# Attention and a gated feed-forward block in one kernel: whole-array value matmuls for two batches, loads tied to TensorE's place in the list, and a new list

## The chip, the cores and the metric

The kernel runs on one core of one Trainium2 chip. The metric is the time of one execution on the device in microseconds (us). A core has five engines that work through queues of their own: TensorE (PE in the profile; its weight loads are listed apart as PEld), VectorE (DVE), ScalarE (ACT), GpSimd (POOL) and SyncE (SP). Matrix results land in PSUM, everything else on the core lies in SBUF. Transfers are carried by 16 DMA engines and are issued here from three places: POOL's queue (loads, which also turn float32 into bfloat16), SP's queue (transposing transfers and stores), and ACT's (one load and one store).

## The reference

```python
def _attn_ref(q, k, v, beacon_k, beacon_v):
    # q, k, v: (8, 8, 576, 64); beacons: (8, 8, 16, 64)
    k_all = np.concatenate([beacon_k, k], axis=2)
    v_all = np.concatenate([beacon_v, v], axis=2)
    scores = scale * np.matmul(q, k_all.transpose(0, 1, 3, 2))
    ...
    scores = np.where(causal, -1000000000.0, scores)
    scores = scores - scores.max(-1, keepdims=True)
    a = np.exp(scores)
    a /= a.sum(-1, keepdims=True) + 1e-09
    return np.matmul(a, v_all).astype(np.float32)

def _moe_ref(x, w_gate, w_val, w_out):
    # x: (4608, 512); w_gate, w_val: (512, 1536); w_out: (1536, 512)
    g = x @ w_gate
    silu = g * (1.0 / (1.0 + np.exp(-g)))
    val = x @ w_val
    return (silu * val @ w_out).astype(np.float32)
```

`scale` is 1/8. The mask is causal over the 576 tokens; the 16 beacon keys in front of them are seen by every query. The attention output, with the eight heads side by side, is the `x` of the feed-forward block.

## The kernel before, in words

**Attention** goes by batch (8) and by pair of heads (4 per batch). The 592 keys are cut into five blocks of 128 rows (`NKT`), the 576 queries into five blocks (`QBLOCKS`). Scores are made transposed, keys on the partitions and queries along the row, in four units per pair (`UNITS`), each into one PSUM slot of two banks, one bank per head. `exponent` (line 323) takes a unit to SBUF as bfloat16, in tiles `p0` to `p2`; `mask` (line 330) zeroes the diagonal blocks on DVE or POOL, unless the scores were masked already by a few extra matmuls. `pv` (line 348) multiplies the exponentials with the values `vb`, which have a column of ones as a 65th column, so that the sum of a row falls out beside its result. `normalize` (line 366) divides on DVE and writes `x`.

**Queries and keys** must have the head dimension on the partitions. Batches 0 to 2 (`NPE`) are loaded as runs of rows, regrouped (`regroup`), transposed on TensorE (`turn`) and copied out of PSUM (`turned_copy`). Batches 3 to 7 are loaded in row blocks and transposed by transfers from SP (`dma_transposes`, line 272, ten per batch). `x` of batch 0 is transposed on TensorE (`x_turn`), that of the others by five or six transfers from SP (`x_transpose`, line 392).

**Feed-forward** goes by chunk of 512 tokens (9) and block of 128 of the 1536 features (12). `gate_value` (line 404) makes gate and value of a block in one slot of two banks, in two pieces of 8 matmuls; `tanh`, `act1` and `act2` build the activation on ACT and DVE; `project` (line 444) multiplies with `w_out`, two matmuls a piece; `evacuate` copies the result to SBUF and stores it.

**Row halves.** Nearly every matmul of TensorE goes through `halves` (line 112): it uses 64 of the 128 rows of the array, and two in a row use the two halves and run together, each writing a bank of its own. When a bank that one half has written is to be written by the other, a `nop` on TensorE waits for the last matmul of that slot before (the "gate"). `pv` is called twice for a pair. The first call takes the upper half of the keys for one head and the lower half for the other; the second call swaps them. Each call issues 30 matmuls of 64 rows by 128 columns of weights with 65 moving columns: for each of the 15 combinations of query block and key block, two.

**The order** is written out by hand in strings (`plan`, line 615), one letter for each piece of work; `piece` (line 560) turns a letter into instructions, and each engine takes its own in that order. The letters that matter here: S/s scores, without and with masking matmuls, E exponential, D/M mask on DVE/POOL, P/p first and second call of `pv`, R normalize, T transpose, c/C regroup, K/k/Q/q copies of transposes, X/Y/y batch 0's `x`, V `x_transpose`, t one transfer of `dma_transposes`, g gate matmuls of the first block as soon as parts of `x` are there, G/H the two gate pieces, a/1/2 activation, F one `project` piece, O/o `evacuate` on DVE/ACT, h two filling matmuls that are issued with the next scores or values, and l the next load. Loads are issued from POOL in the order of the list `loads` (119 of them); POOL also works on the masks M, in the same queue. A load waits until its buffer is free, and, since eight semaphores are used in turn for POOL's transfers, until the load eight places earlier has landed. The buffers `qk`, `vb`, `qT` and `kT` are double.

Of the kernel before, what the change touches and what calls it, by code (L numbers as in the profile page):

```python
# [55 lines left out]
def kernel(  # L56
# [52 lines left out]
    def give(key):  # L109
        spare.append(held.pop(key))  # L110

    def halves(key, bank, row, o, l, r, start, stop, turn=False):

        at = (held[key], bank)
        was = writers.get(at)
        if was is not None and was[0] != row:
            last = max((w for (i, _), w in writers.items() if i == at[0]), key=lambda w: w[2])
            if was[3]:
                gate = nc.tensor.nop()
                tc.add_manual_dep(  # L120
                    gate.ins,
                    last[1],
                    mybir.DependencyInfo(mybir.DependencyClass.Sync, mybir.DependencyReason.DATA),
                    reason="one bank, two row halves",
                )
            for other, w in writers.items():
                if other[0] == at[0]:
                    writers[other] = (w[0], w[1], w[2], False)
        if turn:
            ins = nc.tensor.transpose(o, l, r)  # L130
        else:
            ins = nc.tensor.matmul(o, lhsT=l, rhs=r, start=start, stop=stop)  # L132
# [408 lines left out]
    loads = [  # L541
        weights[1], vl[0][2], vl[0][5], vl[0][3], vl[0][0], vl[0][4], vl[0][1], run_loads(1)[1], weights[0],
        run_loads(1)[0], lambda: beacon_load(1), vl[1][4], weights[3], vl[1][3], weights[2], weights[5],
        vl[1][1], vl[1][2], weights[4], weights[7], vl[2][0], weights[6], vl[1][5], vl[1][0],
        lambda: load_wo(1), lambda: load_wo(0), run_loads(2)[1], run_loads(2)[0], lambda: beacon_load(2),
        vl[2][1], vl[2][2], vl[2][4], vl[2][3], vl[2][5], kl[3][0], kl[3][1], ql[3][0], kl[3][2], ql[3][1],
        kl[3][3], ql[3][2], kl[3][4], ql[3][3], kl[3][5], ql[3][4], kl[4][0], kl[4][1], ql[4][0], kl[4][2],
        ql[4][1], kl[4][3], ql[4][2], kl[4][4], ql[4][3], kl[4][5], ql[4][4], vl[3][0], vl[3][1], vl[3][2],
        vl[3][3], vl[3][4], vl[3][5], kl[5][0], kl[5][1], ql[5][0], kl[5][2], ql[5][1], kl[5][3], ql[5][2],
        kl[5][4], ql[5][3], kl[5][5], ql[5][4], vl[4][0], vl[4][1], vl[4][2], vl[4][3], vl[4][4], vl[4][5],  # L550
        kl[6][0], kl[6][1], ql[6][0], kl[6][2], ql[6][1], kl[6][3], ql[6][2], kl[6][4], ql[6][3], kl[6][5],
        ql[6][4], vl[5][0], vl[5][1], vl[5][2], vl[5][3], vl[5][4], vl[5][5], kl[7][0], kl[7][1], ql[7][0],
        kl[7][2], ql[7][1], kl[7][3], ql[7][2], kl[7][4], ql[7][3], kl[7][5], ql[7][4], vl[6][0], vl[6][1],
        vl[6][2], vl[6][3], vl[6][4], vl[6][5], vl[7][0], vl[7][1], vl[7][2], vl[7][3], vl[7][4], vl[7][5],
    ]
# [59 lines left out]
    plan = [
        "0TclqKTlKhslEsQlEsclcTElsKTEslKElhhsQlQEhhslEslEslEslEslhhhhhPElspEsRPESplPREspERsXlEXDXyPyYpgRl",
        "cXlcyTlcTqgKqTKlGaqKlSHE1G2acslHE1T2aGQklG1lS2HElDGaDSH1E2lSaHDE1G2aGlD1SlHE2HaDlG1al2Gl1SHE2HaD",
        "G1al2G1SHE2saDPHE12pasRPlEp1SFEF2FFFFRsFEslFFEDSFFPEspEDsFRFlFEFFclPcTplcqTKFFlkFFRTqFlFkFFcVSlq",
        "FOFFEFlTOFFFKlqSFFEDSlFFFEMSFlFFFEDSlFESDlFPFEMSplFERFSFMtFFlESOGolEGMDtSHMElGtaDlS1HEtl2HaltG1a",
        "M2Gtl1SHEl2tGlaDl1StHEl2HatMGl1at2Gl1SHE2HlaGM1a2G1SHE2HaDG1a2SHEt1MGa2tP1P2tplpRlSHtElRSaFtlFFE",  # L620
        "1SFlF2FtEFSFlDPDFEDtSlpEDSFRlFtFESFMFPlEtSFpMEDSFltFERSFlFFEFSlFFMDFESVFMFFlFoPlFoFpEMSRFESFlFFF",
        "DESDFPEFMSplFRFESMFEFFFDlSFDEStPlFFEpltGRlGtlSHEltGal1HVl2Hal1Gal2FFH1l2lGaOloG1MSMH2EMGlaDSt1lH",
        "E2lHtaGl1at2Gl1MStHE2HaMtG1at2G1SHE2MGa1SHE2HaMG1al2Gl1SHlE2HlaDG1al2Gl1SHlE2HlaG1la2Gl1SlHE2MGa",
        "D1PH2paGRH1Ga2H12Ga1SHE2HaDG1a2G1SHE2HaDS1aFFF2EFFF1SFEtFMF2FFMFPtFFpStRFESFFFFtEDSFFFFEMSFtFOFF",
        "oFFDFEFFDFFtFFPPtppRSlFtEFFlFRSFEStlFFFFElSFVFFFlEOSFoFPlESFMpMFERSMFFFESFDFFDPDEMSFDEpSFRFEMSFF",
        "FESDtFFFFPEMtFDGptGRHtGat1H2Hta1Gat2FFH1o2GatOG1SH2EtGaDtS1HE2HtaMG1a2G1SHE2HaMG1a2G1SHE2GaD1SHE",
        "2HaMS1FaFFE2FFFF1FSF2ESFFFDPEDFFMpSRlFESFlFFFVEDSlFFFFEDlSFFFFoOlFFDPElFDFpSRFESFFFFEDSPFEFMpSFR",
        "FEMSFEFFDFSFMEGGMSHEHaMG1a2FFH1G2a1G2FHOGOa1SHE2MGa1FFFF2FFHGa1H2Ha1Ga2FFH12Ga1G2HGa1FFFF2HFaFH1",
        "FaF2FFF1FFF2FFFOFFFFOPPppRSFEFFFRSFMESFFVPEDSFpFEDSFMESRFFFFEMSFFFFEDSFFOFFoFPDESFDEpSFRFEMSFFFE",
        "SDFFPFEDGMpGRHGa1H2Ha1Ga2FFH12Ga1G2HGa1FFFF2FFFPFFpoOHRGaV1H2Ga1H2Ga1FH2Ha1Ga2FFF1G2HHa1Ga2FFH12",  # L630
        "Ga1G2HGa1H2Ha1Ga2FFH12Ga1G2HGa1H2Ha1Ga2FFF1G2FHGa1FFFF2FFFFFFFFFOHOFaFFG1F2FFFFFFFHGa1FFFF2FFFFF",
        "FFFFoOFFFFFFHGa1H2Ha1Ga2FFF1G2FFHGa1H2Ha1Ga2FFH12Ga1G2FFFFFHGa1H2Ha1Ga2FFF1G2FFHooGaFF1FFF2FFFFF",
        "FFHFaFH1FaF2FFF1FFF2FFFoFFFoFFFFFFFFFFFFFFFFFFFFFOFFOFFFFFFFFFoFFFFoFFFFFFFFoO",
    ]
# [40 lines left out]
```

## Time and profile before

| what | value |
|---|---|
| median of 3 runs (range) | 388.66 us (385.17 to 393.87) |
| profiled execution, its own time | 392.0 us |
| its span (first to last instruction) | 389.5 us |
| mean granted TensorE clock | 0.969 of full |
| TensorE matmul busy | 360.5 us, 5338 matmuls |
| VectorE / ScalarE / GpSimd busy | 227.9 / 186.0 / 122.7 us |
| packets of loads (POOL's queue) | 95,424, 18.85 MB |
| packets of transposes and stores (SP's queue) | 48,224, 19.92 MB |
| packets of instructions (TensorE's) | 41, 0.67 MB |

The page gives the busy time of each engine, the span in 40 equal slices with a digit for the busy share of each (and rows for the granted clock and the DMA engines), the share of each DMA queue, and the chain of work that ended last: the way back from the last instruction, at each step to what released it. In the lists of waits a line names the waiting engine and its line, then what ended the wait, then microseconds in total, how often, and the longest. "Issue" stands where the profile shows nothing that was waited for. A table of windows gives, for each stretch of time, its length and mean, the busy microseconds of each engine with the number of instructions, the clock, the DMA share (over 1 when packets overlap) and the gigabytes per second moved.

### The profile page before, as it was taken

The page shows a single profiled execution, that of the slowest core. Times are in us where ns is not written, and L with a number is a line of the kernel's source. Part 1 is how long each engine was busy: PE and PEld are TensorE (multiplying, and loading weights), DVE is VectorE, ACT ScalarE, POOL GpSimd, SP SyncE. Part 2 cuts the span into 40 slices and gives each one's busy share as a digit, 9 for nine tenths or more (in the row PEclk, how much of TensorE's full clock was granted, in tenths as well). Part 3 has the DMA queues.
Part 4 walks back from the last instruction along what each step waited for, and adds up shares of the span by engine and source line. Part 5 has one row for each costly group of instructions (what it writes and reads, how often), then busy time and mean ns, then how long its engine had stood idle before and what let it go on. Part 6 is the DMA issues. An engine that isn't in the chain of part 4 may idle for free.

```text
span 389.5 us, 12163 instructions
## 1 busy us (share of the span) xinstructions
PE 360.5 (93%) x5338; PEld 206.5 (53%) x5338; DVE 227.9 (59%) x413; ACT 186.0 (48%) x271; POOL 122.7 (31%) x197
## 2 busy tenths in 40 slices
PE   6659999999977689999998999999999999999996
PEld 3455456555544435555665556555665555555543
DVE  4524887747952337778444875477646767456521
ACT  2833667776464526545473567633552332122321
POOL 8754526095664747550171015200100000000000
PEclk9885999999998989999999999999999999999999
DMA  8999999399999999990799618910330400110112
GB/s 152 157 194 194 203 176 126 42 153 164 145 128 142 172 115 185 123 109 0 133 104 160 139 17 71 112 56 2 89 84 2 108 10 0 56 56 2 54 56 109
DMA packets 143989, 39.90 MB, mean 102 GB/s; under 512 B 130368, under 2 KB 139328, under 8 KB 143936
## 3 DMA queue, kind: packets, MB, share of 16 engines
q0 software_dynamic: 95424, 18.85, 66.1%
q1 hardware_dynamic: 48224, 19.92, 29.8%
q8 instruction: 41, 0.67, 0.8%
q10 hardware_dynamic: 288, 0.36, 0.3%
q14 instruction: 12, 0.10, 0.1%
HBM read 38.27 MB, written 9.44 MB: 122 GB/s over the span
## 4 chain that ended last, share of the span: by engine, by line
PE 82%; DMA 6%; issue 4%; POOL 3%; DVE 2%; SPq 2%; ACT 1%; POOLq 0%
PE gv_ps L132 45%; PE o_ps L132 23%; PE pv_ps L132 7%; PE s_ps L132 5%; DMA qT<-qk 2%; DMA vb<-in_v_dram 2%; DMA xT<-x 2%; SPq L274 1%; POOL vb L180 1%; DVE o_sb L224 1%; PE t_ps L130 1%; PE xt_ps L386 1%; POOL qk L171 1%; SPq L397 1%; ACT o_sb L222 0%
## 5 line engine op out<-in xcount | busy, mean ns | idle before, releaser
L132 PE MATMUL gv_ps<-xT,wg 64*128 64x512 bf16 x864 | 201.9, 380 | 6.5 <-issue 4.0
L132 PE MATMUL gv_ps<-xT,wv 64*128 64x512 bf16 x864 | 203.3, 380 | 0.0
L327 ACT ACTIVATE p<-s_ps 128x992 bf16<-128x992 f32 (+2 forms) x128 | 105.5, 865 | 72.2 <-PE s_ps L132 66.4
L132 PE MATMUL o_ps<-wo,hT 64*128 64x512 bf16 (+2 forms) x912 | 115.7, 368 | 2.8 <-issue 2.6
L425 ACT ACTIVATE th<-gv_ps 128x512 f32<-128x512 f32 x108 | 64.4, 596 | 90.7 <-PE gv_ps L132 88.3
L429 DVE SCALAR_TENSOR_TENSOR u<-th,gv_ps 128x512 f32<-128x512 f32 x108 | 73.9, 684 | 57.6 <-ACT th L425 57.3
L132 PEld LDWEIGHTS <-wg 64*128 64x128 bf16 x864 | 80.2, 95 | 49.0 <-PE gv_ps L132 3.8
L132 PEld LDWEIGHTS <-wv 64*128 64x128 bf16 x864 | 79.6, 95 | 44.5 <-issue 5.4
L436 DVE SCALAR_TENSOR_TENSOR hT<-gv_ps,u 128x512 bf16<-128x512 f32 x108 | 74.7, 691 | 3.7
L132 PEld LDWEIGHTS <-hT 64*128 64x128 bf16 x912 | 47.0, 94 | 38.0 <-issue 3.5
L340 POOL TENSOR_SCALAR_AFFINE_SELECT p<-p 128x256 bf16<-128x256 bf16 (+2 forms) x62 | 23.3, 396 | 116.9 <-ACT p L327 100.3
L132 PE MATMUL pv_ps<-vb,p 64*128 64x65 bf16 x1920 | 41.7, 193 | 8.8 <-issue 6.5
L132 PEld LDWEIGHTS <-p 64*128 64x128 bf16 x1920 | 38.8, 96 | 18.1 <-issue 7.6
L132 PE MATMUL s_ps<-qT,kT 64*128 64x80 bf16 (+4 forms) x384 | 46.1, 285 | 2.3 <-DMA qT<-qk 1.3
L180 POOL DMA_DIRECT2D vb<-in_v_dram x40 | 33.8, 854 | 19.0 <-DMA qk<-in_k_dram 4.1
L372 DVE RECIPROCAL rec<-pv_ps 128x10 f32<-128x10 f32 x32 | 7.0, 219 | 45.0 <-PE pv_ps L132 44.9
L336 DVE TENSOR_TENSOR p<-p,upper 128x256 bf16<-128x256 bf16 (+2 forms) x71 | 19.0, 287 | 21.8 <-ACT p L327 21.5
L132 PEld LDWEIGHTS <-kT 64*128 64x128 bf16 x384 | 21.9, 96 | 17.4 <-issue 4.9
L373 DVE TENSOR_TENSOR x<-pv_ps,rec 128x640 bf16<-128x640 f32 x32 | 26.4, 824 | 1.2
L224 DVE COPY o_sb<-o_ps 128x512 f32<-128x512 f32 (+1 forms) x20 | 12.9, 666 | 20.4 <-PE o_ps L132 10.5
L180 POOL DMA_DIRECT2D qk<-in_q_dram x25 | 21.6, 864 | 3.8 <-DMA vb<-in_v_dram 2.9
L180 POOL DMA_DIRECT2D qk<-in_k_dram x25 | 21.4, 857 | 4.2 <-DMA vb<-in_v_dram 2.5
(51 smaller groups left out, 104.0 us busy)
## 6 DMA issues: line engine op xcount, KB each, us to landing
out_dram<-o_sb SPq DMA_DIRECT2D x34, 256.0 KB, 2.4
vb<-in_v_dram POOLq DMA_DIRECT2D x24, 128.0 KB, 10.6
qk<-in_q_dram POOLq DMA_DIRECT2D x20, 128.0 KB, 9.2
qk<-in_k_dram POOLq DMA_DIRECT2D x15, 128.0 KB, 8.7
wv<-in_moe_w_val_dram POOLq DMA_DIRECT2D x4, 384.0 KB, 11.7
wg<-in_moe_w_gate_dram POOLq DMA_DIRECT2D x4, 384.0 KB, 10.4
wo<-in_moe_w_out_dram POOLq DMA_DIRECT2D x2, 768.0 KB, 12.8
qk<-in_q_dram POOLq DMA_DIRECT2D x2, 576.0 KB, 12.4
```

The costliest lines, as they stand in the source:

```text
L130: ins = nc.tensor.transpose(o, l, r)
L132: ins = nc.tensor.matmul(o, lhsT=l, rhs=r, start=start, stop=stop)
L180: return nc.gpsimd.dma_start(dst[p0 : p0 + n, c, :, 0:D], src[b, :, r : r + n, :].rearrange("h j d -> j h d"))
L224: eng.tensor_copy(o, i)
L327: nc.scalar.activation(pt[n // 4 % NPT][:, :, c0 : c0 + w], ps[:, :, 0:w], ACT.Exp, scale=0.125)
L336: nc.vector.tensor_tensor(out=ap, in0=ap, in1=upper[:, None, d : d + w].to_broadcast([P, 2, w]), op=ALU.mult)
L340: nc.gpsimd.affine_select(out=ap, in_=ap, compare_op=ALU.is_ge, fill=0.0, base=d, pattern=[[0, 2], [1, w]], channel_multiplier=-1,)
L372: nc.vector.reciprocal(rec[:], o[:, :, :, D : D + 1])
L373: nc.vector.tensor_tensor(out=xs[b][:, :, P * m : P * m + P].rearrange("p c (h d) -> p h c d", d=D), in0=o[:, :, :, 0:D], in1=rec[:].to_br ...
L425: nc.scalar.activation(th[:], gvs[n][0][:, 0, :], ACT.Tanh, scale=0.5)
L429: nc.vector.scalar_tensor_tensor(out=u[:], in0=ths[n][:], scalar=1.0, in1=gvs[n][0][:, 0, :], op0=ALU.add, op1=ALU.mult)
L436: nc.vector.scalar_tensor_tensor(out=hTs[j][:, f, :], in0=gvs.pop(n)[0][:, 1, :], scalar=0.5, in1=ths.pop(n)[:], op0=ALU.mult, op1=ALU.mult)
```

## The change

Three things are changed.

*Value matmuls.* In batches 0 and 1 (`WIDE` = 2), each call of `pv` makes one head of the pair (`side`), with 15 matmuls over all 128 rows of the array and 65 moving columns, instead of 30 over 64 rows. They don't pass through `halves`, so no gate stands between the two calls.

*Loads.* `piece` notes in `passed` the newest matmul after each letter that issued one. From load number 24 on (`FREE_LOADS`), POOL first executes a `nop` that waits for the last but one entry of `passed`.

*The list.* The strings of `plan` and the order of `loads` are new. `loads` now goes by need in natural order: the six loads of the first V, two weight blocks, batch 1's K and Q, and so on. The first block's gate matmuls come in three pieces instead of two. Letters move over the whole list; the amounts of work stay the same but for small shifts between engines (58 to 62 masks D, 22 to 19 masked score units, 10 to 8 fillers).

```diff
+WIDE = 2
+
+FREE_LOADS = 24
...
+    newest = [None]
+    passed = []
...
-                gate = nc.tensor.nop()
-                tc.add_manual_dep(
...
+                after(nc.tensor.nop(), last[1], "one bank, two row halves")
...
+        newest[0] = ins.ins.name
...
         o_ps = pvs[n]
+        if b < WIDE:
+
+            side = int(second)
+            for c, (q0, _) in enumerate(QBLOCKS):
+                for t in range(c + 1):
+                    col = p_col(t, q0)
+                    ins = nc.tensor.matmul(
+                        o_ps[:, side, 68 * c : 68 * c + D + 1],
+                        lhsT=pt[n % NPT][:, side, col : col + P],
+                        rhs=vb[b % 2][:, t, 2 * m + side, 0 : D + 1],
+                        start=t == 0,
+                        stop=t == c,
+                    )
+            newest[0] = ins.ins.name
+            return
...
     loads = [
-        weights[1], vl[0][2], vl[0][5], vl[0][3], vl[0][0], vl[0][4], vl[0][1], run_loads(1)[1], weights[0],
...
+        vl[0][0], vl[0][1], vl[0][2], vl[0][3], vl[0][4], vl[0][5], weights[0], weights[1], run_loads(1)[0],
+        run_loads(1)[1], lambda: beacon_load(1), weights[2], weights[3], weights[4], weights[5], vl[1][0],
...
-    parts = [(0, [(0, 0), (1, 0), (1, 1), (0, 1), (0, 2), (1, 2)], False), (0, [(1, 3), (0, 3)], True)]
+    parts = [(0, [(0, 0), (1, 0), (1, 1), (0, 1)], False), (0, [(0, 2), (1, 2)], False), (0, [(1, 3), (0, 3)], True)]
...
         if kind == "l":
+            if n >= FREE_LOADS:
+
+                after(nc.gpsimd.nop(), passed[-2], "paced load")
             loads[n]()
...
     plan = [
-        "0TclqKTlKhslEsQlEsclcTElsKTEslKElhhsQlQEhhslEslEslEslEslhhhhhPElspEsRPESplPREspERsXlEXDXyPyYpgRl",
...
+        "0TclqKlTqKlhSEslESDlccTESlQTklESKlQESDDEhhsDEsDEslhhhhhPlEpSRPEplSXREsElYSXDlDEsPlpEDslREsyXEgly",
...
     for kind in "".join(plan):
+        before = newest[0]
         piece(kind)
+        if newest[0] != before:
+            passed.append(newest[0])
```

`after(ins, name, reason)` is a new helper that makes `ins` wait for the instruction `name`.

More of the change, by code (lines that the diff above doesn't have):

```diff
@@ L110, in give, with after @@
         spare.append(held.pop(key))
+    def after(ins, name, reason):
+        tc.add_manual_dep(
+            ins.ins,
+            name,
+            mybir.DependencyInfo(mybir.DependencyClass.Sync, mybir.DependencyReason.DATA),
+            reason=reason,
+        )
+    newest = [None]
+    passed = []
     def halves(key, bank, row, o, l, r, start, stop, turn=False):
@@ L118, in halves @@
             if was[3]:
-                gate = nc.tensor.nop()
-                tc.add_manual_dep(
[L121 to L125, printed above, removed]
+                after(nc.tensor.nop(), last[1], "one bank, two row halves")
             for other, w in writers.items():
@@ L353, in pv @@
         o_ps = pvs[n]
+        if b < WIDE:
[9 more added lines that the diff above has]
+                        stop=t == c,
+                    )
+            newest[0] = ins.ins.name
+            return
         for c, (q0, _) in enumerate(QBLOCKS):
@@ L541 @@
     loads = [
-        weights[1], vl[0][2], vl[0][5], vl[0][3], vl[0][0], vl[0][4], vl[0][1], run_loads(1)[1], weights[0],
[L543 to L551, printed above, removed]
@@ L552 @@
-        ql[6][4], vl[5][0], vl[5][1], vl[5][2], vl[5][3], vl[5][4], vl[5][5], kl[7][0], kl[7][1], ql[7][0],
-        kl[7][2], ql[7][1], kl[7][3], ql[7][2], kl[7][4], ql[7][3], kl[7][5], ql[7][4], vl[6][0], vl[6][1],
-        vl[6][2], vl[6][3], vl[6][4], vl[6][5], vl[7][0], vl[7][1], vl[7][2], vl[7][3], vl[7][4], vl[7][5],
+        vl[0][0], vl[0][1], vl[0][2], vl[0][3], vl[0][4], vl[0][5], weights[0], weights[1], run_loads(1)[0],
+        run_loads(1)[1], lambda: beacon_load(1), weights[2], weights[3], weights[4], weights[5], vl[1][0],
@@ new lines @@
+        vl[1][1], vl[1][2], vl[1][3], vl[1][4], vl[1][5], weights[6], weights[7], lambda: load_wo(0),
+        lambda: load_wo(1), lambda: beacon_load(2), run_loads(2)[0], run_loads(2)[1], vl[2][0], vl[2][1],
+        vl[2][2], vl[2][3], vl[2][4], vl[2][5], kl[3][0], kl[3][1], ql[3][0], kl[3][2], ql[3][1], kl[3][3],
+        ql[3][2], kl[3][4], ql[3][3], kl[3][5], ql[3][4], kl[4][0], kl[4][1], ql[4][0], kl[4][2], ql[4][1],
+        kl[4][3], ql[4][2], kl[4][4], ql[4][3], kl[4][5], ql[4][4], vl[3][0], vl[3][1], vl[3][2], vl[3][3],
@@ new lines @@
+        vl[3][4], vl[3][5], kl[5][0], kl[5][1], ql[5][0], kl[5][2], ql[5][1], kl[5][3], ql[5][2], kl[5][4],
+        ql[5][3], kl[5][5], ql[5][4], vl[4][0], vl[4][1], vl[4][2], vl[4][3], vl[4][4], vl[4][5], kl[6][0],
+        kl[6][1], ql[6][0], kl[6][2], ql[6][1], kl[6][3], ql[6][2], kl[6][4], ql[6][3], kl[6][5], ql[6][4],
+        vl[5][0], vl[5][1], vl[5][2], vl[5][3], vl[5][4], vl[5][5], kl[7][0], kl[7][1], ql[7][0], kl[7][2],
+        ql[7][1], kl[7][3], ql[7][2], kl[7][4], ql[7][3], kl[7][5], ql[7][4], vl[6][0], vl[6][1], vl[6][2],
@@ L555 @@
+        vl[6][3], vl[6][4], vl[6][5], vl[7][0], vl[7][1], vl[7][2], vl[7][3], vl[7][4], vl[7][5],
     ]
     turns = [load for b in range(NPE, B) for load in dma_transposes(b)]
-    parts = [(0, [(0, 0), (1, 0), (1, 1), (0, 1), (0, 2), (1, 2)], False), (0, [(1, 3), (0, 3)], True)]
+    parts = [(0, [(0, 0), (1, 0), (1, 1), (0, 1)], False), (0, [(0, 2), (1, 2)], False), (0, [(1, 3), (0, 3)], True)]
     wholes = 1
@@ L615 @@
     plan = [
-        "0TclqKTlKhslEsQlEsclcTElsKTEslKElhhsQlQEhhslEslEslEslEslhhhhhPElspEsRPESplPREspERsXlEXDXyPyYpgRl",
[L617 to L630, printed above, removed]
@@ L631 @@
-        "Ga1G2HGa1H2Ha1Ga2FFH12Ga1G2HGa1H2Ha1Ga2FFF1G2FHGa1FFFF2FFFFFFFFFOHOFaFFG1F2FFFFFFFHGa1FFFF2FFFFF",
-        "FFFFoOFFFFFFHGa1H2Ha1Ga2FFF1G2FFHGa1H2Ha1Ga2FFH12Ga1G2FFFFFHGa1H2Ha1Ga2FFF1G2FFHooGaFF1FFF2FFFFF",
-        "FFHFaFH1FaF2FFF1FFF2FFFoFFFoFFFFFFFFFFFFFFFFFFFFFOFFOFFFFFFFFFoFFFFoFFFFFFFFoO",
+        "0TclqKlTqKlhSEslESDlccTESlQTklESKlQESDDEhhsDEsDEslhhhhhPlEpSRPEplSXREsElYSXDlDEsPlpEDslREsyXEgly",
+        "PpgRcXlycTlcTkgQlTkQGlacGk1qHl2TaGKqH12SlaHE1G2aGlD1SlHE2HaDG1a2G1slH2ElSHaEG1la2slHE1lG2laDGl1s",
@@ new lines @@
+        "2HElsaHE1G2asHE1S2aPlpE1sl2EsRPEpsDFRFElSFEFFFsPDEpsRFEslFFFcFEFcTFcTkPQpklcTqFRlFFkTFFKVlSFEFQF",
+        "FlFFqDSFOlFESFOFlFFEDSFFlFFEDSFESDFPFEDSlpFlERFSFFMtFFElSFEGltMGMtSHMEHtaDlG1alt2FFHl1tG2al1Gtl2",
+        "HltGal1Ht2lHatl1Ga2lFFHl1OlGaOHl21Ga2Gl1SH2EGlaDSH1El2lSaHDE1G2laSHE1MS2laPDPEl1p2lpRSFlEtFFFFRM",
+        "SFtESFlFDFFEDSltPFEFDptMSFRESltFFEFMFFStPMESFplEDtSFRFFlFESlVFDESFFDlFFoDFFFloFFFESlFESFMPFFEMpS",
+        "MRFESFFFFEDSFFlFFEtDSFPOoMGEpMtGRHtGat1PH2tpaGRltH1GaV2H12Gal1SHE2lHaDGl1a2Gl1SlHEt2lHatlG1a2Glt",
@@ new lines @@
+        "1SMHE2ltHaMtG1al2Gtl1SHE2ltGaM1SHlE2HlaDG1al2G1lSHE2HaDG1a2Gl1SHlE2HalG1aM2Gl1SHE2lGaM1SlHE2HlaG",
+        "1Mal2G1lSHE2lHaMG1al2G1SHE2HaDSF1aFFFE2FFMF1FFF2PFFpSRFESFFFFEMSFFFFEMSFtFFFEMOFFoFFMPPtppRSFtEF",
+        "FFRSFMEStFFPEDSFtpFEMRSFEStFlFFMFEDSFlVFFFESMFFlOFFESFOESlFFDFFESDlFDFFFESMPlFFEDpMSRFESFFFFEMSP",
+        "tFEFDptSFRFEMGtDFGooHGat1Ht2Ga1Ht2Gat1SHE2tHaDG1at2G1tSHE2HtaMG1at2G1StHE2HtaDG1a2G1SHE2GaD1FFFH",
+        "2Ha1PaFF2pF1SFEF2FFFRFMSPEFFpDSRlPEFFplVSFRESFMFEFFDlFSFESFMFOFlFESFOFFlFEDSFDESFlFDFPEMSFpEDSFR",
@@ new lines @@
+        "FFFEMSFDEFGDGSHEHaMG1a2FFH1G2a1G2HGa1H2Ha1Ga2FFH12Ga1G2HGa1H2Ha1Ga2FFH1o2oGaSP1EH2MpaSFRFEFFMFF1",
+        "FSFES2FFFFEMSPFEFMpSFRFESFEFFDFVSFDMESFFFFEDSFOFFFoDFFFEFFMFFPFFpSRFESFFFFEDSFPEFDSpFRFEGFDGOHOG",
+        "Da1H2Ga1H2Ga1H2Ga1PH2paGRH1Ga2H12Ga1H2Ga1FFFF2FFFPHpaHRFaFF1VG2FF1G2HHa1FaFFF2FFF1FFF2FFFOFFFFOF",
+        "FFFFFGGFHGa1FFFF2FFFFFHGa1H2Ha1Ga2FFH12Ga1G2HGa1FHo2oHaGa1G21H2Ga1FFFF2FFFFHGa1FFFF2HGa1H2FaFFG1",
+        "F2FFFFFFFFFoOFFFFFFFFFFFHGa1H2Ha1Ga2FFH12Ga1G2HGa1H2Ha1Ga2FFH12Ga1G2FFFFFFFFFOoFFFFFFFFFFFHGa1H2",
@@ L634 @@
+        "Ha1Ga2FFF1FFF2FFFFFHFaFOFFoFF1FFF2FFFFFFFFFFFFFFFFFoOFFFFFFFFFFFoFFFFoFFFFFFFFOo",
     ]
     for kind in "".join(plan):
+        before = newest[0]
         piece(kind)
+        if newest[0] != before:
+            passed.append(newest[0])
     NU = NF * NCH
```

## The prediction

> **What bounds the kernel now.** I read the page's busy times and slices first, then TensorE's own waits, then the chain of waits in order of time.
>
> ```profile
> PE 360.5 (93%) x5338; PEld 206.5 (53%) x5338; DVE 227.9 (59%) x413; ACT 186.0 (48%) x271; POOL 122.7 (31%) x197
> ...
> PE   6659999999977689999998999999999999999996
> ...
> PEclk9885999999998989999999999999999999999999
> DMA  8999999399999999990799618910330400110112
> ...
> q0 software_dynamic: 95424, 18.85, 66.1%
> q1 hardware_dynamic: 48224, 19.92, 29.8%
> q8 instruction: 41, 0.67, 0.8%
> ```
>
> No engine but TensorE (PE) comes near the span. Its slices (9.7 us each) are low in two places, 0 to 29 us and 107 to 146 us, in both of which the clock digit falls too and the DMA digit is 9. The last queue carries instructions: 10,719 weight loads, matmuls and events on PE against 42 packets (one after the end) are 255 each, so a packet of 16 KB is 256 instructions. Those packets pass through the same engines as the loads.
>
> ```profile
> PEld L132 <- issue: 24.5, 34, 4.2
> ...
> PE pv_ps L132 <- issue: 6.5, 4, 3.5
> PE gv_ps L132 <- issue: 4.0, 1, 4.0
> PE o_ps L132 <- issue: 2.6, 1, 2.6
> PE pv_ps L132 <- DMA vb<-in_v_dram: 2.2, 1, 2.2
> ```
>
> "Issue" is time in which PE waited for nothing that the profile shows. I set the instruction packets beside it: a packet runs at 23.8 to 25.0, 119.4 to 120.3, 126.7 to 127.9 and 135.5 to 136.8 us, and PE resumes about 1.4 us after each end. So issue is PE out of instructions. The chain has the places:
>
> ```profile
> 11.98 8.03 DMA vb<-in_v_dram
> 20.06 0.62 PE pv_ps L132 x27
> ...
> 23.11 3.45 issue
> ...
> 32.08 0.68 issue
> ...
> 46.66 1.73 PE gv_ps L132 x16
> ...
> 61.99 0.46 PE pv_ps L132 x30
> ...
> 111.73 1.41 issue
> ...
> 119.13 2.58 issue
> ...
> 128.27 1.00 issue
> ...
> 134.22 3.96 issue
> ```
>
> The six issues sum to 13.1 us. The chain also gives PE's prices at full clock: 16 gate matmuls 1.73 us (8 make a piece, 0.86), 30 value matmuls 0.46. Two output matmuls (512 columns, together) are 0.216, which is 2.4 columns per ns, and scores are their columns at that rate. Adding these prices along the list gives 341.3 us of PE work, so the span of 389.5 holds 48.2 of loss. Laying the same sum beside the actual starts dates the loss: 15.0 us behind at the first value matmul (20.1 us), 24.9 at 39.7, 25.6 at 56, 26.6 after the first gate of chunk 1 (82), 28.2 at 108, 41.0 at 141, 43.1 after 208, 45.3 at 385, and 2.9 for the last stores. Two stretches cost 9.9 and 12.8 us.
>
> ```profile
> 20.00:30.00 10.00, 6.49 (x235) 6.02 (x236) 3.33 (x7) 4.23 (x6) 5.05 (x7) 0.79 1.49 194
> 30.00:40.00 10.00, 9.00 (x148) 4.71 (x148) 4.74 (x9) 3.28 (x7) 4.62 (x7) 0.52 1.53 193
> ```
>
> In this table of windows (PE first; then PEld, DVE, ACT, POOL, clock, DMA, GB/s) PE is nearly busy from 30 to 40, at half clock: the clock is 0.5 from 25.9 to 39.5 us, and again for 3.4 us at 121.4 and at 138.5. The first is about 6 us of the 9.9.
>
> **What the Trainium skill says.** "TensorE: Matmul & The Clock Gate", Part 1, What's actually happening: an idle window of about 3.4 us halves PE's clock. The trace agrees: the three half-clock stretches last 13.65, 3.41 and 3.41 us, and each follows stalls of 2.6 to 4 us. The same page, Part 3, The mechanism, says that weight loads overlap running matmuls only in other row groups; taken alone that would expose each load of a whole-array matmul. The trace disagrees: the six 128-column warm-up matmuls on the whole array start 56 ns apart, which is their streaming time, each with its own weight load. "TensorEngine Tiling (Array Packing)", Key Properties: a change of tiling mode drains the array. Here the start after a whole-array transpose comes some 0.13 us late at half clock. "DMA: Bandwidth & Descriptors", Queues, rings and completion order: each DMA engine takes packets round robin from its queues; this fits the late instruction packets, whose own transfer takes only 0.9 to 1.5 us.
>
> **The change part by part.**
>
> *Whole-array value matmuls, batches 0 and 1.* 8 pairs x 60 become 8 x 30: 240 matmuls and 240 weight loads fewer. Two half-array matmuls run together now, 30 in 0.46 us, 31 ns a pair. A whole-array one streams the same 65 columns. The trace has none so short, so bounds: 27 ns (65 columns at that rate) if the load hides, 56 ns (the 128-column interval) if it doesn't. For 240 that is -0.8 to +6 us; I take 30 ns, nothing, because half-array loads already pass every 15 ns. The array changes mode about 16 more times at 0.07 to 0.13 us: +1.1 to 2.1; the removed gates between row halves give some back; I take +1.0. What the part buys is instruction packets: 480 fewer, nearly two of 42, all where PE consumes fastest.
>
> *Order of the first loads.* Before, a weight block (384 KB) is ahead of V, and the first value matmul waits for V until 20.06. Now V's six loads lead. At 150 GB/s the block is 2.6 us, so V lands near 17.5, with 4.1 us of PE work before it: lag 13.4 instead of 15.0. Batch 0's 16 exponentials (13.7 us of ACT from 9.8) then end near 24.5, not 29.9, because three of them no longer wait behind V and the issue.
>
> *Instruction packets at the start.* In the trace a packet comes 5.5 to 8 us after PE has used some 0.65 of the block before, and 1.1 blocks (280 instructions) then cover it. Before, PE used 280 between 20.9 and 23.1 us. In the new list that takes 5.4 us, so 3.45 and 0.68 shrink to about 0.5, and the half-clock stretch that began there (6 us) should not begin. Next late are batch 1's Q and K: behind V and two weight blocks, issued near 15 and landing 11 us later, then 0.7 of regrouping; their transposes stand at 12.3 of the list, 26 us. I put +2 us there. Lag 16 at list time 15, where it was 24.9.
>
> *Paced loads.* POOL now waits for PE's piece two back before each load from number 24 on. Behind such a wait stand POOL's later loads and its masks, and the value matmuls wait for those. From number 45 on the old loads already ran within 4 us of PE's place in the list, held by masks, so there the wait binds little. Numbers 24 to 43 ran 11 us ahead and lose that. Batch 2's Q and K: listed at 28.5, regrouped at 42.2, 13.7 us; landing took 12 to 16 us in that stretch: +1. Batch 3's ten K/Q loads now lie over 39 to 53 in the list, on top of batch 1's x transposes at 46.7 on SP's queue; before, DMA share was 0.58 from 66 to 78 us and those landed in 4.5 us, against 9 under load. The fourth of five is needed 8.2 us after the first issue; 4 issues x 1.3 plus 6 to 7 is near 12: 3.5 us of wait where there was 1.0.
>
> *Attention of batches 3 and 4* (list 80 to 105). These value matmuls stay half-array. Instructions in list time 75 to 100 fall from 1,246 to 1,179, and 280 of them span 6.0 to 6.9 us for all packets there, against 5.5 to 6.1 for the first two that stalled. Latency was 6 to 8, so stalls shrink to 3 or so. But batch 2's x transposes follow 8.0 us after their issue begins; under load they need 4 x 1.4 plus 9, 14.6. Before, the stalls in between hid that (the lag grew about 6 us meanwhile). With fewer stalls the wait shows: I take 3 of stalls, 3.5 of x, 1 of clock: 7.5 for 12.8.
>
> *After that* nothing differs much: 1.4 at batch 4's x, 0.5, 1.8 at the end, 2.9 of stores.
>
> Sum: work 341.0 + mode changes 1.0 + 16 + 1 + 3.5 + 7.5 + 1.4 + 0.5 + 1.8 + 2.9 = 376.6 us of span, 12.9 less. The profiled execution took 392.0 for its span of 389.5; it was 3.3 over the median 388.66, so I carry the difference over: 388.7 - 12.9 = 375.8, say **376**.
>
> **The rivals.** *More:* pacing frees the engines enough that both the x waits and the stalls of batches 3 and 4 go: 7.5 and 3.5 become 3 and 1, run loads on time saves 2: 9 less, 367. For it: the instruction packets themselves are short. Against: the bytes stay the same, 133 GB/s for loads and transposes in that stretch alone where 126 to 169 were moved.
>
> *Nothing measurable:* PE still gets throttled at the start by small waits (+6), the x waits take their full 5.5 and 11 for 3.5 and 7.5 (+5.5): 387. For it: four half-clock windows were needed to recover though PE was nearly busy. Against: the 3.45 us hole that set it off has a cause that the list removes.
>
> *Slower:* pacing feeds back. A load waits for PE, PE for the load, and POOL can no longer use a stall to run ahead. Batches 2 to 7 have six sets of loads; if each lands 3 us late and costs 1.7 of half clock, 28 us are added: 404. It decides once landing exceeds the list distance to the user; for batch 3 that is 12.6 us from last load to last transpose, and 15 was seen. Against: from number 45 on the old kernel lived with the same distances.
>
> **How the numbers follow.** Forecast 0.53, more 0.17, nothing 0.20, slower 0.10. The 80% range leaves out about half the "more" case and the "slower" one: 366 to 388. A change under 2% (7.8 us) can't be told from none here: faster 0.70, same 0.20, slower 0.10.
>
> **What would show it.** Right: first value matmul near 17.5 us, no issue over 1 us before 40, clock 1.0 from 25 to 40, PE at batch 1's first gates 8 us earlier, the share of issue in the chain from 4.0% to about 1.5%, and a wait of gate matmuls for xT or a DMA near 70 and near 115 us. Wrong: value matmuls at over 45 ns each, idle PE on turn or qk loads near 58 us, POOL waiting on PE with TensorE idle at the same time, or a throttled start for another reason.

## The result, and the profile after

| | before | after |
|---|---|---|
| median (range) | 389.63 us (385.17 to 395.78) | 384.1 us (381.94 to 387.37) |
| profiled execution, its own time | 392.0 us | 384.61 us |
| span | 389.5 us | 382.9 us |
| mean granted TensorE clock | 0.969 | 0.973 |
| TensorE stalled for instructions (issues over 0.6 us, set beside the packets) | 13.1 us | none |
| gate matmuls waiting for transposed `x` | 1.3 us | 12.2 us |

The ratio is 0.9896, with a 95% interval of 0.9865 to 0.9928: 1.0% faster, well short of the 3.3% forecast and inside the 2% that was to count as no change. The ratios, here and below, are taken from each kernel's fast runs alone (some executions lie over 1.5% above its fastest), so they are not the quotients of the medians beside them. The page of the profile after:

```profile
span 382.9 us, 11703 instructions
...
PE 359.4 (94%) x5090; PEld 202.2 (53%) x5090; DVE 227.4 (59%) x412; ACT 187.3 (49%) x275; POOL 122.1 (32%) x195
...
PE   7789999689997799999979999999999999999995
...
PEclk9699999969999899999998999999999999999999
DMA  8999999999999979991896509501420311010113
...
q8 instruction: 40, 0.66, 0.7%
```

The dip of before at 10 to 29 us is shallower (digits 7 and 8 where 6 and 5 stood), and the long hole from 107 to 146 is gone. Three short ones stand in its place, at slices 8, 13 to 14 and 21, and with or just behind each the clock digit falls as well. What TensorE waits for there is in the table of waits (waiting engine and line, what ended the wait; us in total, times, longest):

```profile
PEld L143 <- issue: 20.9, 33, 5.3
POOL qk L192 <- issue: 15.2, 9, 11.4
...
POOL qk L192 <- PE gv_ps L143: 10.9, 3, 7.2
PE gv_ps L143 <- DMA xT<-x: 9.3, 2, 5.2
...
PE gv_ps L143 <- issue: 2.8, 1, 2.8
```

The first line is mostly the waits of the last two, seen from the weight loads: 4.6, 5.3 and 3.3 us of it lie at the same three places. The fourth line is two waits of gate matmuls for `x`, 4.16 us at 73.5 and 5.19 us at 121.8. The last, at 197.9, is put down to "issue", but batch 4's third transpose was issued at 193.2 and took 7.5 us to land, which is 200.7, when TensorE went on: it is a wait for `x` too. The third line is new: loads of POOL that wait for TensorE's gate matmuls, which is the pacing. The chain of waits after, in order of time, around the first two places:

```profile
65.76 0.64 SPq L424
...
66.45 1.33 SPq L424
...
67.82 1.34 SPq L424
...
69.20 8.30 DMA xT<-x
...
77.64 3.60 PE gv_ps L143 x16
...
116.97 2.03 SPq L424
...
119.05 7.82 DMA xT<-x
...
127.01 1.89 PE gv_ps L143 x8
```

Each `x` transpose takes SP some 1.3 us to issue and lands 7 to 8 us after its issue began, and TensorE needs the third or fourth of five. The 16 gate matmuls at 77.64 take 3.60 us where the prediction's price at full clock is 1.73: the wait has halved the clock. The trace shows half clock from 75.6 to 82.4, 126.8 to 130.2 and 201.9 to 205.3 us, once after each of the three waits, and 10.7 to 17.5 at the start. These stretches last 3.4 or 6.8 us, once or twice the window that the Trainium skill names in "TensorE: Matmul & The Clock Gate", Part 1, What's actually happening. That page asks for a whole idle window before the clock is halved; here a wait of 2.80 us was enough, and shorter ones are in the last section.

Laying the list's prices beside the actual starts, as the prediction did for before, dates TensorE's lag behind its list:

| stretch | lag forecast | lag measured |
|---|---|---|
| first value matmul | 13.4 (at 17.5 us) | 13.8 (at 17.9 us) |
| before chunk 1 (54.6 in the list) | 17 | 18.9 |
| chunk 1 | +3.5 | +6.65 |
| attention of batches 3 and 4, chunk 2 | +7.5 | +6.85 |
| chunk 4 | +1.4 | +4.6 |
| the rest, without the stores | +2.3 | +1.2 |

### The profile page after: what moved, and what is told of

It is laid out like the page before. It is cut to its first block, busy times and chain, and to the rows that moved or that the text cites. A ratio compares the mean times of both kernels' runs of the same rounds, so it can differ in the third digit from the quotient of the medians.

```text
span 382.9 us, 11703 instructions
## 1 busy us (share of the span) xinstructions
PE 359.4 (94%) x5090; PEld 202.2 (53%) x5090; DVE 227.4 (59%) x412; ACT 187.3 (49%) x275; POOL 122.1 (32%) x195
## 4 chain that ended last, share of the span: by engine, by line
PE 85%; DMA 6%; DVE 3%; ACT 2%; SPq 2%; issue 1%; ACTq 0%; DVEq 0%
PE gv_ps L143 50%; PE o_ps L143 20%; PE s_ps L143 5%; PE pv_ps L143 5%; DMA xT<-x 4%; SPq L424 2%; PE pv_ps L372 2%; PE idle_ps L546 2%; DMA qk<-in_q_dram 1%; ACT p L339 1%; PE t_ps L141 1%; DVE qT L236 1%; DVE turn L236 1%; ACT kT L234 1%; DVE x L400 0%
## 5 line engine op out<-in xcount | busy, mean ns | idle before, releaser
L143 PE MATMUL o_ps<-wo,hT 64*128 64x512 bf16 (+2 forms) x912 | 112.8, 365 | 0.2
L143 PEld LDWEIGHTS <-wv 64*128 64x128 bf16 x864 | 80.5, 95 | 41.3 <-issue 2.2
L192 POOL DMA_DIRECT2D vb<-in_v_dram x40 | 33.7, 847 | 17.9 <-PE gv_ps L143 3.8
L143 PEld LDWEIGHTS <-p 64*128 64x128 bf16 x1440 | 28.2, 95 | 7.1 <-issue 0.5
L143 PEld LDWEIGHTS <-kT 64*128 64x128 bf16 x384 | 21.0, 96 | 16.8 <-DVE x L400 1.8
L143 PE MATMUL pv_ps<-vb,p 64*128 64x65 bf16 x1440 | 29.6, 191 | 0.1
L192 POOL DMA_DIRECT2D qk<-in_q_dram x25 | 21.3, 852 | 12.9 <-PE gv_ps L143 7.2
L236 DVE COPY o_sb<-o_ps 128x512 f32<-128x512 f32 (+1 forms) x20 | 12.9, 668 | 18.5 <-PE o_ps L143 12.3
## 6 DMA issues: line engine op xcount, KB each, us to landing
wg<-in_moe_w_gate_dram POOLq DMA_DIRECT2D x4, 384.0 KB, 10.7
qk<-in_k_dram POOLq DMA_DIRECT2D x2, 576.0 KB, 10.7
```

The lines of the kernel that those rows point to most:

```text
L192: return nc.gpsimd.dma_start(dst[p0 : p0 + n, c, :, 0:D], src[b, :, r : r + n, :].rearrange("h j d -> j h d"))
L236: eng.tensor_copy(o, i)
```

## The experiments

Medians are of this kernel and of the kernel before on the same chip; the ratio has its 95% interval.

| run | what it is | us | before | ratio (interval) |
|---|---|---|---|---|
| a_fill | after, filling matmuls ahead of three waits | 382.49 | 390.47 | 0.9845 (0.9782 to 0.9907) |
| a_unpaced | after without pacing | 378.9 | 390.47 | 0.9732 (0.9655 to 0.9808) |
| a_narrow | after, value matmuls all on half arrays | 388.05 | 390.47 | 1.0017 (0.9969 to 1.0064) |
| a_away | after, loads out of the way of transposes | 380.19 | 390.47 | 0.9778 (0.9706 to 0.9849) |
| b_wide | before + whole-array value matmuls alone | 380.62 | 390.14 | 0.9774 (0.9718 to 0.983) |
| b_paced | before + pacing alone | 391.45 | 390.14 | 1.002 (0.9989 to 1.0051) |
| b_natural | before + new order of loads alone | 387.78 | 390.14 | 0.9951 (0.9923 to 0.9979) |
| d_list | after, half arrays and no pacing | 379.35 | 391.68 | 0.9735 (0.9673 to 0.9796) |
| d_wide5 | before + whole array in batches 0 to 4 | 378.59 | 391.68 | 0.9696 (0.9635 to 0.9758) |
| c_split | a_away, whole array in 0 to 4, batch 4's `x` in two parts | 371.03 | 390.14 | 0.9507 (0.9466 to 0.9548) |
| d_split_unpaced | c_split without pacing | 371.32 | 391.68 | 0.952 (0.9469 to 0.9571) |
| d_split8 | c_split, whole array in all batches | 376.03 | 391.68 | 0.9638 (0.9587 to 0.9689) |

The theory was that pacing puts loads on top of the transposes of `x`, that these land late, and that each wait costs its length and then half clock. Its rivals: the waits would come anyway once the stalls for instructions are gone (the transposes are late because TensorE is early), or the whole-array matmuls are themselves dearer than was priced.

### Half clock after the waits: a_fill

Filling matmuls (16, 20 and 10 pairs) stand ahead of the first gates of chunks 1, 2 and 4, so that TensorE isn't idle while it waits. They write what the gate matmuls overwrite.

```diff
+FILL = {1: 16, 2: 20, 4: 10}
...
+            if f == 0 and j in FILL:
+                for _ in range(FILL[j]):
+                    for row in range(2):
+                        r = slice(HALF * row, HALF * row + HALF)
+                        nc.tensor.matmul(
+                            gvs[n][0][:, row, :], lhsT=wo[r, 0, 0:P], rhs=wo[r, 0, :], start=True, stop=True
+                        )
```

> The changed kernel with filling matmuls ahead of the first gate matmuls of chunks 1, 2 and 4: 16, 20 and 10 pairs of 512 columns into the same slot (3.5, 4.3 and 2.2 us), which the gate matmuls overwrite. Theory 1: TensorE waits there 4.2, 5.2 and 2.8 us for the x transposes, and each wait also costs half a clock afterwards (6.8, 3.4 and 3.4 us at 0.5, in all 5.7 us of lost work). Then the fillers take no time of their own, the clock stays at 1.0 from 70 on, and the span falls by about 5 us against the changed kernel. Rival: what follows the waits is bound by something other than TensorE's clock, or the x transposes land just in time in most runs; then the time is the same, or up to 3 us longer by fillers that outlast the wait.

The half-clock stretches at the three places are gone. With the filling left out of the sum, the lag grows by 4.2 us at chunk 1 and 2.8 at chunk 4, where after has 6.65 and 4.6: that difference is the price of the half clock. But against after the median fell by only 1.6 us, not the 5 expected, and the two intervals overlap. The chain of this kernel says where the gain went:

```profile
109.87 0.21 PE o_ps L145 x2
110.08 0.21 PE pv_ps L145 x11
110.29 2.45 issue
112.74 0.42 PE pv_ps L145 x16
```

In the middle of a run of value matmuls TensorE ran out of instructions, 2.45 us, with half clock from 114.0 to 117.4 after it. The lag, 23.5 at list time 75 where after has 25.7, had grown to 28.3 by 94, where after has 26.2. So TensorE came earlier to batch 3's value matmuls, and a stall that after doesn't have there took most of the gain back.

### Pacing: a_unpaced and b_paced

```diff
-FREE_LOADS = 24
+FREE_LOADS = 119
```

> The changed kernel with no load held to TensorE's place in the list; all else as changed. Theory 1 (the pacing lays batch 3's loads over batch 1's x transposes): those land in 4 to 5 us instead of 7.5 to 8.3, the wait before chunk 1's gates goes from 4.2 to 1 us and its half clock (2.3 us) with it; the other two waits stay; -5 us, if no stall for instructions comes back. Theory 2 (pacing is what ended the stalls for instructions): stalls of 1 to 4 us each return where loads run ahead, 5 us or more in all, and the time is equal or longer than the changed kernel's.

Without pacing the changed kernel is 378.9 us: pacing costs 5 to 6 us in this list, and the interval lies clear of after's. (The trace is of an execution of 383.2 us, the five others took 375.8 to 379.8, so places are read from it and not totals.) Batch 1's transposes from 60 to 84 us, first in the changed kernel, then without pacing:

```profile
L424 SPq DMA_TRANSPOSE xT<-x x5: 1288/1330/2246, 65.1 to 71.5; - x5
...
DMA to landing us min/median/max: 6.8/7.5/8.3
```

```profile
L424 SPq DMA_TRANSPOSE xT<-x x5: 1267/1286/1827, 65.4 to 70.8; - x5
...
DMA to landing us min/median/max: 3.7/5.5/6.5
```

They are issued at the same time by both kernels and land 2 us sooner without pacing. TensorE reached chunk 1's gates at the same time too (73.5 and 73.8 us) and waited 0.52 us instead of 4.16, and no half clock followed. The windows of 73 to 84 us, after and then unpaced (length; busy us of PE, PEld, DVE, ACT, POOL; clock; DMA share; GB/s):

```profile
73.00:84.00 11.00, 6.84 (x44) 2.85 (x40) 0.69 (x2) 2.70 (x4) 3.68 (x8) 0.69 1.66 189
```

```profile
73.00:84.00 11.00, 10.48 (x100) 5.29 (x98) 4.88 (x9) 4.41 (x7) 9.86 (x16) 1.00 1.83 161
```

That settles the wait at chunk 1: TensorE was no earlier, the transposes were later, and pacing made them so. The DMA share of these windows is no smaller without pacing; what differs is where the loads lie. Between 65 and 73 us seven loads are issued with pacing and three without, and from 69 to 75 us, while the fourth transpose is on its way, the DMA share is 2.23 with pacing and 1.36 without. It is not the whole of it. Unpaced, stalls for instructions are back (2.04 us at 103, 2.71 at 110.6 and 2.51 at 128.7, 7.3 in all), and batch 2's `x` is later still (8.5/8.9/10.0 us to landing), yet only 1.79 us of that shows, since two of the stalls lie ahead of it. So both theories on record were right in part: pacing did hold these stalls off, and cost more than they do.

Pacing alone on the kernel before:

```diff
+FREE_LOADS = 24
...
+            if n >= FREE_LOADS:
+                after(nc.gpsimd.nop(), passed[-2], "paced load")
...
+        before = newest[0]
...
+        if newest[0] != before:
+            passed.append(newest[0])
```

> The kernel before with the pacing alone (loads from number 24 on wait for TensorE's piece two back), old list, half arrays. If pacing costs as it does in the new list (there 5 us): batch 3's loads move from 55 to 64 us into 66 to 78 us, over batch 1's x transposes, whose landing goes from 4.5 to 7 us or more, and chunk 1's gates wait 3 to 5 us instead of 0.8, with half a clock after it: +3 to +7 us. If pacing helps the instruction packets: the stalls between 111 and 134 us (9 us in all) shrink, -3 to -8 us.

```profile
PE pv_ps L145 <- issue: 9.3, 4, 3.9
PE gv_ps L145 <- DMA xT<-x: 4.7, 2, 4.1
```

It makes no difference in time. The 3 to 7 us expected did not come. The wait of chunk 1 is there with the same size (4.06 us at 83, half clock 86.3 to 89.7), and its transposes take 5.7/7.5/8.3 us to land where the kernel before had 2.5/4.5/5.2. What it gives in exchange is shorter stalls for instructions in the attention of batches 3 and 4: 1.23, 2.50 and 0.99 us, where before had four with 8.95 in all. Those at the start (3.90 and 1.42 us) are not shorter, and one of 1.45 at 67 is new.

### Whole-array value matmuls: a_narrow, b_wide, d_wide5

```diff
-WIDE = 2
+WIDE = 0
```

> The changed kernel with all value matmuls on half arrays again (240 matmuls and 240 weight loads more, gates between the calls back). If fewer instructions at the start are what ended the stall of 3.45 us and the half clock behind it: a stall of 1 to 3.5 us between 18 and 30 us and up to 6 us of half clock return, +3 to +9 us. If the earlier V loads and the list did it: no stall; value matmuls 0.045 us shorter per call (0.46 for 0.505), 16 calls, -0.7 us, within 1 us of the changed kernel.

With half arrays the changed kernel is no faster than before. The start stays good (first value matmul at 17.7 us, no stall before 40), so the list, the order of loads and the pacing together mend the start without the whole-array matmuls. But at batch 1's attention, in the chain of this kernel:

```profile
61.26 0.32 PE pv_ps L143 x10
61.58 2.60 issue
64.18 0.48 PE pv_ps L143 x20
```

a stall with half clock from 64.8 to 68.2, and the waits for `x` of chunks 1 and 2 on top (4.45 and 4.51 us).

The other way round, the same edit alone on the kernel before, for batches 0 and 1 and then for 0 to 4:

```diff
+WIDE = 2
...
+        if b < WIDE:
...
+            return
```

> The kernel before with one part of the change alone: whole-array value matmuls in batches 0 and 1 (WIDE = 2), old list, no pacing. If TensorE's use of instructions at the start is what outruns their packets: 240 fewer matmuls and weight loads, so the stall of 3.45 us at 23 us shrinks to 2 or less and the half clock from 26 to 39.5 us shortens; -3 to -8 us against before. If the late V loads set the start, because several calls wait for V and then run in a row: the stall stays and the time is within 1.5 us.

> The kernel before with whole-array value matmuls in batches 0 to 4, old list, no pacing. With batches 0 and 1 alone it ran at 380.6 and still stalled 2.6 (for instructions), 2.6 and 1.8 us between 108 and 128. If instructions outrun their packets there too, those go with their half clock (1.7), whole arrays cost 1.1 us, and the x wait of chunk 2 shows (1 to 5 us, since the stalls hid it): 374 to 379. Rival: the x wait takes the place of the stalls in full: 380 to 382.

What TensorE waits for longest in b_wide:

```profile
PE pv_ps L134 <- POOL p L342: 2.6, 1, 2.6
PE o_ps L134 <- issue: 2.6, 1, 2.6
PE pv_ps L362 <- DMA vb<-in_v_dram: 2.3, 1, 2.3
PE pv_ps L134 <- issue: 1.8, 1, 1.8
```

This one part alone takes 2.3% off, more than the whole change does, and five batches 3.0%. With two batches the stall of 3.45 us at 23 is gone though list, loads and V (first value matmul at 19.56) are as before; half clock at the start lasts 3.4 us, not 13.65. Three stalls of 2.60, 2.64 and 1.77 us stay in batches 3 and 4 (the first line is one of them: it lies at the same place of a packet as the others, as told under "Instruction fetches" below). With five batches those are gone, and a wait of 3.21 us for `x` at 122.7 with half clock behind it stands there instead: the same exchange as in the changed kernel.

### The order of loads, and the list: b_natural, d_list

```diff
-        weights[1], vl[0][2], vl[0][5], vl[0][3], vl[0][0], vl[0][4], vl[0][1], run_loads(1)[1], weights[0],
...
+        vl[0][0], vl[0][1], vl[0][2], vl[0][3], vl[0][4], vl[0][5], weights[0], weights[1], run_loads(1)[0],
...
```

> The kernel before with the new order of loads alone (V's six first, then two weight blocks, batch 1's K and Q), old list, half arrays, no pacing. The first value matmul comes near 17.5 us instead of 20 where TensorE is ready for it (17.9): -2 us. If the bunching of value matmuls behind V caused the stall at 23 us, the stall goes too, with the half clock: -8 to -12 us. If the stall is only a matter of their number: it stays and the sum is -2 us or nothing.

The order alone is worth 0.5%. The start has stalls of 2.47 and 1.14 us and 3.4 us of half clock; of before's later stalls most stay, in smaller pieces.

```diff
-WIDE = 2
+WIDE = 0
...
-FREE_LOADS = 24
+FREE_LOADS = 119
```

> The changed kernel with neither whole arrays nor pacing: the new list and the new order of loads alone. If the parts add up: 378.9 without pacing, and half arrays cost 4 us in the paced list, so 383, 1.8% under before. If half arrays cost as much as they do in the old list (9.5 us): 388, about 0.5% under before.

TensorE's waits for instructions and for `x` in this kernel:

```profile
PE pv_ps L143 <- issue: 4.0, 4, 1.8
PE o_ps L143 <- issue: 2.6, 1, 2.6
PE gv_ps L143 <- DMA xT<-x: 0.3, 1, 0.3
```

The new list with its order of loads, without the other two parts, takes 2.65% off, more than either expectation (383 or 388 us) allowed. It has stalls of 1.35 us at 24, 1.80 at 106 and 2.61 at 114.5, and no wait for `x` over 0.8 us. Adding the whole-array matmuls (a_unpaced, 0.9732) changes nothing that can be measured, and adding pacing to that loses more than half of it. In this list pacing costs more with half arrays (0.9735 to 1.0017, a_narrow) than with whole ones (0.9732 to 0.9896): the whole arrays earn something here only where pacing stands.

### Loads out of the way: a_away, c_split, d_split_unpaced, d_split8

Pacing kept, but letters `l` moved: loads 34 to 43 earlier, ahead of batch 1's transposes, and 69 to 78 and 107 to 112 behind the first gates of chunks 2 and 4. The first of the strings:

```diff
-        "2HElsaHE1G2asHE1S2aPlpE1sl2EsRPEpsDFRFElSFEFFFsPDEpsRFEslFFFcFEFcTFcTkPQpklcTqFRlFFkTFFKVlSFEFQF",
...
+        "2HElsaHE1G2asHE1S2aPlpE1sl2EslRPlEplslDFlRFlESlFlEFlFlFsPDEpsRFEsFFFcFEFcTFcTkPQpkcTqFRFFkTFFKVS",
...
```

> The changed kernel with loads moved out of the way of three sets of x transposes: batch 3's (numbers 34 to 43) 2 to 8 us earlier in the list, batch 4's and 5's numbers 69 to 78 and batch 6's V (107 to 112) behind the first gates of chunks 2 and 4. Theory 1 (x transposes land late because loads share the DMA engines with them): they land in 3 to 5 us instead of 6 to 8, the waits of 4.2, 5.2 and 2.8 us fall to about 1 each and the half clocks go: -10 to -14 us; with only half the effect -5. Rival (the x transposes are bound by their issue on SP, 1.3 us apiece, and by other transposes in that queue): landing stays above 6 us and the time within 2 us.

All three waits for `x` are gone: batch 2's transposes land in 2.4/4.3/5.7 us (after: 7.1/7.4/7.8), batch 4's in 2.4/2.5/4.0 (4.9/5.9/7.5). Against after the median fell by 3.9 us, not by the 10 to 14 expected; the trace is of the fastest of six executions (376.1 us, the others up to 381.1). Stalls for instructions of 0.82 and 1.84 us at 103 and 109.5 are back, and one new wait stands in the table, with its origin in the chain:

```profile
PE s_ps L143 <- DMA qT<-qk: 4.3, 1, 4.3
```

```profile
184.71 1.97 SPq L424
...
186.73 1.27 SPq L424
...
188.04 1.25 SPq L424
...
190.48 1.22 SPq L286
...
191.79 7.95 DMA qT<-qk
```

On SP's queue batch 6's transposes of Q and K (L286) stand behind six transposes of batch 4's `x` (L424); the scores of batch 6 wait 4.30 us, and half clock follows for 3.4. So c_split issues the last of batch 4's `x` row blocks behind batch 6's transposes, by a new letter v, and takes the whole array for batches 0 to 4:

```diff
-WIDE = 2
+WIDE = 5
...
-    def x_transpose(b):
+    def x_transpose(b, rest=False):
...
+            if b == 4 and rest != (c > 2):
+                continue
...
+        elif kind == "v":
+            x_transpose(4, True)
```

> The kernel with the loads moved out of the way, and two more edits: whole-array value matmuls in batches 0 to 4 (WIDE = 5), and batch 4's x transposes that chunk 4 doesn't need (row blocks 3 and 4) issued behind batch 6's last transposes on SP. In the run before it, TensorE waited 4.3 us at 195 us for batch 6's transposes, queued behind batch 4's x, and stalled 0.8 and 1.8 us at 103 and 109. Theory: the first wait falls to under 1 us with its half clock (-5 us), the stall and wait at 103 to 110 go; whole arrays cost 0.09 us per pair more, 12 pairs, +1.1 us. Against the run before it -4 to -6, that is 375. Rival: something else is late next and the time stays at 379 to 381.

```profile
PE 357.2 (97%) x4730; PEld 196.5 (53%) x4730; DVE 227.2 (61%) x412; ACT 187.5 (51%) x275; POOL 122.1 (33%) x195
...
PE   7698999999999999999998999999999999999996
...
PEclk9799999999999999999999999999999999999999
```

371.03 us, 4.9% under before and the fastest kernel of the study, 9 us under a_away where 4 to 6 were expected. After 20 us there is one wait over 0.5 us left (1.18 at 199.4), and no half clock at all. Does it need the pacing?

```diff
-FREE_LOADS = 24
+FREE_LOADS = 119
```

> The fastest kernel so far (loads out of the way, x of batch 4 split, whole arrays in batches 0 to 4) without pacing. If pacing is bad wherever it stands, as it was in the changed kernel: -2 to -5 us against 371. If it only hurts by where the list put the loads: with the loads out of the way of the x transposes it does no harm, and without it loads run ahead into them again (numbers 69 to 78 are held back by nothing but masks): +1 to +5 us.

No: 371.32 us, with intervals that lie over each other. In this list loads stand where they harm no transposes, and pacing neither helps nor hurts.

```diff
-WIDE = 5
+WIDE = 8
```

> The fastest kernel so far with whole arrays in all batches (WIDE = 8). No stall for instructions is left there, so only the price is: 3 batches, 12 pairs, 0.09 us each for streaming and about 0.1 us for each change of the array's mode: +1 to +3 us against 371. If stalls come back in some runs, -1.

With the whole array in all batches it is 5.0 us slower, more than the 1 to 3 expected, though it has 360 matmuls fewer. The growth is not a wait: from 209 to 290 us the same output and gate matmuls fall behind those of c_split by 4.25 us, in steps of 0.21, one at each of the 20 calls of `pv` there. The chains show the step. A whole-array call between output matmuls in c_split, and half-array calls between output matmuls in the changed kernel:

```profile
102.65 0.56 PE pv_ps L372 x15
103.21 0.54 PE o_ps L143 x4
103.75 0.56 PE pv_ps L372 x15
```

```profile
196.06 0.45 PE pv_ps L143 x30
196.51 0.43 PE o_ps L143 x4
196.94 0.46 PE pv_ps L143 x30
```

From the first start to the last the 15 matmuls take as long as the 30 (0.43 us in both traces), and 0.1 us is added on going to the whole array and 0.1 on coming back. That fits the drain on a change of mode that the Trainium skill states in "TensorEngine Tiling (Array Packing)", Key Properties; the price is this trace's. The 24 calls of batches 5 to 7 by 0.21 are 5.0 us, the difference of the medians. The two traces lie 5.5 us apart; what else differs in them nets to 0.5 (two waits of 1.5 and 1.3 us at 62 and 75 in d_split8 against the one at 199.4 in c_split).

## Why the prediction was wrong

**Instruction fetches: the cause right, the cure in part.** That the six stalls are instruction packets that come late holds, and more firmly than the prediction could say. Of the 32 waits over 0.6 us that the fourteen traces put down to issue, 30 lie at place 193 to 195 of a block of 256, counting TensorE's weight loads, matmuls and events from the kernel's start, whatever the work there; the other two are chunk 4's gates waiting for `x`. (Three waits put down to other engines, at 110.6 us in a_unpaced, 109.5 in a_away and 117.1 in b_wide, lie at these places too.) 13.1 us of stalls became none, and that the start's long half clock goes with the stall holds (clock 1.0 from 25 to 40 us). That fewer instructions end a stall is shown where the matmuls were halved (b_wide, d_wide5). In batches 3 and 4 of the changed kernel they were not halved: the forecast allowed 3 us of stalls there and none was left, but in the trace without pacing there are 7.3, close to the 8.95 of before. There it was pacing that held them off, which only the rival "more" had counted on.

**Start: right.** V landed as forecast, and the lag before chunk 1 was 18.9, against 17 plus the 1.0 that was put down for mode changes: 0.9 over.

**Whole-array value matmuls: right.** Within a call they start 30 to 31 ns apart, where 30 was taken, and a change of mode costs 0.1 us, inside the 0.07 to 0.13 forecast. A pair of calls with scores around it takes 1.13 to 1.33 us against 1.36 to 1.39 on half arrays, whose second call waits for a gate. A call that stands alone among half-array matmuls costs 0.21 us more; the change has none of those.

**Paced loads: the step that failed.** It named the place (batch 3's loads on top of batch 1's transposes), the mechanism and nearly the landing ("under load 9", measured 6.8 to 8.3), and then sized the wait at 3.5 us at chunk 1 and a total of 1 us for half clock. Measured at chunk 1 are 4.16 us of wait and 2.5 of half clock; at chunk 2 5.19 and 1.7; and at chunk 4, which "nothing differs much" covered with 1.4, 2.80 and 1.8. Chunks 1 and 4 together are 6.35 us over, the whole of the 6.3 by which the span (382.9) missed the sum (376.6); the small misses elsewhere cancel. That 7.5 came near the 6.85 measured at chunk 2 is luck: the 3 us of stalls in it did not come, and wait and half clock together were 2.4 over their 4.5. Two errors lie in this step. First, half clock was priced into the stalls of before, where it was seen, and not into the waits that were to replace them, though every wait of 2.8 us or more in these kernels, whatever it was for, had half clock behind it. How much came depends on chance as well: see the grid in the last section. Second, the new list at chunk 4 was taken to be as good as the old: there the wait is 1.33 us before, 1.95 in the new list without pacing and 2.80 with it, and half clock follows the last two and not the first. So at chunk 4 pacing is a part only. What makes up the rest stays open: the same list with half arrays and without pacing (d_list) waits 0.74 us there.

**The rivals.** "Nothing measurable" (387) had its waits for `x` in full right at chunk 1 (6.65 us for its 5.5) but not at chunk 2 (6.85 for its 11), and its throttled start wrong: there is no half clock from 17.5 to 75 us. "Slower" named the feedback that was found, at three places instead of six; at chunk 1 it cost some 4 us of wait and 2.5 of half clock, and a_unpaced, with 0.52 us of wait and no half clock there, shows that pacing was the cause. "More" failed because pacing relieved the packets but loaded the transposes.

**Profile and median.** The forecast carried 12.9 us from one profiled execution to the median. The profiled execution of before took 392.0 us, 2.4 over the median of 389.6 that more runs gave; that of after was 0.5 over its own. So the profiles differ by 7.4 us and the medians by 5.5, and 1.9 us of the shortfall is in this step.

What stays open: why pacing holds off stalls for instructions (the packets' own transfer takes about 1 us in all kernels, and which of the loads delays a packet wasn't tried), what pacing does beside whole arrays in the old list, and how c_split does with the whole array in two batches only, which would save some of its mode changes.

## What to carry to other kernels

When a stall is removed, look up which transfer is needed next at the engine's new, earlier time, and price the wait for it together with the half clock that follows a wait of this length; here that was half as much again. To hold loads back until TensorE has got somewhere says nothing about what else uses the DMA engines at that moment: with ten loads placed ahead of the transposes that they hit, and sixteen behind, it made no difference whether the others were held back. Run the parts of a composed change one by one: here each of two parts alone gained twice what the whole did, together they gained no more than one (both take away stalls for instructions), and the part that lost was hidden by them.
